# One padded column buffer, and the order of two transposes in front of the seventh pair, in a retention and mixture-of-experts kernel

## The chip, the cores and the metric

The kernel runs on one core of a Trainium2 chip. The metric is the device time of one launch in microseconds. Three runs of the kernel before took 415.46, 417.1 and 418.48 us; the median is 417.1 us.

## The reference

Two stages, all in float32. First a retention (linear attention) over 4 batches, 8 heads, 768 steps and head size 64:

```python
state = gamma * state + einsum('bhd,bhe->bhde', k[t], v[t])
y[t] = scale * einsum('bhd,bhde->bhe', q[t], state)
```

Its output is read as x, 3,072 tokens of 512 numbers. Then a mixture of 8 experts: each token goes to the expert with the largest logit x @ w_gate, and gets

```python
h = maximum(x[mask] @ w1[e], 0)            # 512 -> 1024
out[mask] = gate_w * sigmoid(x @ w_output_gate)[e] * (h @ w2[e])
```

## The kernel before, in words

**Attention, the first 125 us or so.** The 768 steps of a batch are cut into 6 chunks of 128. Two batches run beside each other, so the 24 chunks make 12 *pairs* (`for p in range(NCH // 2)`), the chunks of pair p being `n0 = 2p` and `n1 = 2p + 1`. Pairs 0 to 5 work on the first two batches, pairs 6 to 11 on the others. `nxt = p + 1`, and `NC` is 6, so `nxt == NC` holds once, at the end of the sixth pair (p = 5), in front of the seventh.

For each pair TensorE does, in this order: `inter` (queries by the state of the chunks before; left out where a batch starts, so in the seventh pair too), `scores` (L399, keys by queries), transposes of a part of the queries for a later pair, `tokens` (L529, outputs turned for the router), `values` (L417), `state` (L424, left out at a batch's last chunk), `counts` (L490 to L495), and then, for the next pair, `turn_keys` twice (L346) and `turn_queries` (L359), and at the end `logits` (L443). ScalarE copies most of the transposed tiles out of PSUM (`keep_keys`, `keep_queries`, both with L342, the line of the helper `copy`). With `nxt == NC` the second chunk's keys are copied by VectorE.

PSUM is handed out by hand: four banks `sp[0]` to `sp[3]`, named s0 to s3 below. Two habits matter here. `scores(n0)` of an even chunk writes banks s0 and s1, `scores(n1)` writes s2 and s3; the turned queries stand in s1 until ScalarE has copied them, the turned keys in s2 and s3; and the small sums of `gates` (VectorE, L516 to L520) stand in a corner of s0, since `gates(grp, bank[:, 6 * E:6 * E + 4])` is called with `bank = sp[0]`.

The order of each engine's instructions is the order of the program text (`tc.manual_schedule()`): no planner moves anything.

**Loads.** `load_k` (L273), `load_v` (L278), `load_q` (L283) and `first_queries` (L312) are issued by SyncE (queue 1), two by ScalarE at the start. A chunk of k or v is 256 KB: to each of 128 partitions, 8 heads of 64 floats, so 8 pieces of 256 bytes. `load_q` takes two chunks, in pieces of 512 bytes. Each waits for a free buffer (6 for k, 4 for v, 2 for q).

**Experts, from there to the end.** Tokens are sorted by expert through DRAM (`scatter`, L556), each expert's tokens are read back, split into a high and a low part (`xh`, `xw`) and multiplied with w1 (L1048), the result (`hh`, `hl`) with w2 (L1071, L1099). Weights come in slices of 512 KB into five buffers `raw`, each 1,056 floats = 4,224 bytes a partition, one behind the other: w1 as 4 pieces of 512 bytes per partition, w2 as one piece of 2,048. As 4,224 is 16 x 256 + 128, the five start by turns at a multiple of 256 bytes and 128 behind one.

**Where buffers lie.** The pools are stacked in the order in which they are opened: constants, weights, `hpool`, and behind it the attention's pools, and later, in the attention's place, the experts' pool. In `hpool` stand `col0` (7 numbers used, 32 taken), and behind it `idx0`, `tmp0` and `ot0`. Whatever lies behind `col0` moves if it grows; `raw`, `whi`, `wlo`, `xh0`, `xw0` and `h0` lie ahead of it.

Of the kernel before, what the change touches and what calls it, by code (L numbers as in the profile page):

```python
# [13 lines left out]
I32 = mybir.dt.int32  # L14
# [8 lines left out]
HEAD = 224  # L23
# [11 lines left out]
def retention_moe_kernel(  # L35
# [15 lines left out]
    P = 128  # L51
# [4 lines left out]
    NC = S // P  # L56
# [12 lines left out]
    hpool = ctx.enter_context(tc.tile_pool(name="hpool", bufs=1))  # L69
# [177 lines left out]
    with ExitStack() as actx:  # L247
# [6 lines left out]
        sp = [ps_s.tile([P, 512], F32, name=f"s{b}") for b in range(4)]  # L254
# [83 lines left out]
        def blocks(bank):  # L338
            return bank.rearrange("p (g t) -> p g t", g=NG)

        def copy(eng, dst, src):
            (eng.copy if eng is nc.scalar else eng.tensor_copy)(dst, src)  # L342

        def turn_keys(i, bank):
            for g in range(NG):
                nc.tensor.transpose(blocks(bank)[:, g], kn[i][:, 2 * g:2 * g + 2].rearrange("p h d -> p (h d)"), ident)  # L346

        def keep_keys(i, bank, eng=nc.scalar):
            kt[i] = ap.tile([P, NG, P], F32, name="kt", tag="kt", bufs=2)
            copy(eng, kt[i], blocks(bank))  # L350
# [5 lines left out]
        def turn_queries(ch, j, r, bank):  # L356
            src = qr.pop((ch, j, r))
            for g in range(NG):
                nc.tensor.transpose(blocks(bank)[:, g], src[:, 2 * g:2 * g + 2].rearrange("p h d -> p (h d)"), ident)  # L359
# [13 lines left out]
        def keep_queries(ch, j, r, bank, eng=nc.scalar):  # L373
            if r == 0:
                qt[ch, j] = ap.tile([P, NG, 2, P], F32, name="qt", tag=f"qt{ch}", bufs=2)
            copy(eng, qt[ch, j][:, :, r], blocks(bank))
# [108 lines left out]
        def counts(grp, bank):  # L485
            n = len(grp)
            oh = rt["oh"]
            cnt = bank[:, 0:n * E]
            rt["cnt"] = cnt
            nc.tensor.matmul(cnt, tri_b, oh.rearrange("p a e -> p (a e)"), start=True, stop=False, skip_group_check=True)  # L490
            for t in (cb, acc):
                nc.tensor.matmul(cnt.rearrange("p (a e) -> p a e", e=E), ones_b, t.unsqueeze(1).broadcast_to([P, n, E]),
                                 start=False, stop=True, skip_group_check=True)
            if n == 2:
                nc.tensor.matmul(cnt[:, E:2 * E], ones_b, oh[:, 0], start=False, stop=True, skip_group_check=True)  # L495

        def add_counts(grp, eng):
            for a in range(len(grp)):
                eng.tensor_tensor(out=acc, in0=acc, in1=rt["oh"][:, a], op=ALU.add)

        def route2(grp, bank):
            n = len(grp)
            oh = rt.pop("oh")
            rk = bank[:, 4 * E:6 * E].rearrange("p (a e) -> p a e", a=2)
            nc.vector.tensor_tensor(out=rk, in0=rt.pop("cnt").rearrange("p (a e) -> p a e", e=E), in1=oh, op=ALU.mult)
            pos = sm.tile([P, 2], I32, name="pos", tag="pos", bufs=4)[:, 0:n]
            with nc.allow_low_precision("row numbers are whole"):
                nc.vector.tensor_reduce(out=pos, in_=rk, axis=AX.X, op=ALU.add)  # L508
            for a, i in enumerate(grp):
                rt["pos", i] = pos[:, a:a + 1]  # L510

        def gates(grp, tmp):
            ex = rt.pop("ex")
            n = len(grp)
            se, den = tmp[:, 0:2], tmp[:, 2:4]
            nc.vector.tensor_reduce(out=se, in_=ex[:, :, 0:E], axis=AX.X, op=ALU.add)  # L516
            nc.vector.tensor_scalar(out=se, in0=se, scalar1=1e-9, scalar2=None, op0=ALU.add)
            nc.vector.scalar_tensor_tensor(out=den, in0=ex[:, :, E], scalar=1.0, in1=se, op0=ALU.add, op1=ALU.mult)
            gate = sm.tile([P, 2], F32, name="gate", tag="gate", bufs=3)[:, 0:n]
            nc.vector.reciprocal(gate, den)  # L520
            for a, i in enumerate(grp):
                rt["gate", i] = gate[:, a:a + 1]
# [31 lines left out]
        def scatter(i, last=False, mark=None):  # L554
            row = rt.pop(("row", i))
            s_ = nc.gpsimd.indirect_dma_start(  # L556
                out=srt, out_offset=bass.IndirectOffsetOnAxis(ap=rt.pop(("pos", i)), axis=0),
                in_=row.rearrange("p a x -> p (a x)"), in_offset=None, bounds_check=E * REG - 1, oob_is_err=False)
            wait_for(s_, mark)
            if not last:  # L560
                tc.declare_no_dep(s_.ins, group="srt", reason="rows are disjoint")
                tc.add_to_no_dep_group("srt", s_.ins)
            else:
                for o in sent:
                    tc.add_manual_dep(s_.ins, o.name, mybir.DependencyInfo(
                        mybir.DependencyClass.Sync, mybir.DependencyReason.DATA), reason="sorted rows complete")
            sent.append(s_.ins)
# [18 lines left out]
        hd = {}  # L586
# [18 lines left out]
            nc.gpsimd.tensor_sub(hd["xl"][:, 2 * g:2 * g + 2], tp, hd["xh"][:, 2 * g:2 * g + 2].bitcast(F32))  # L605

        def keep_ids():
            hd["c"] = hpool.tile([P, 32], I32, name="col0")[:, 0:HEAD // 32]
            nc.gpsimd.tensor_copy(hd["c"], hd["t"][:, :, P].bitcast(I32))

        def head_ids():
# [98 lines left out]
        for p in range(NCH // 2):  # L710
# [3 lines left out]
            nxt = p + 1  # L714
            ahead = (p % 2, p // 2 + 1) if 2 <= p < 2 * NQ - 2 else None
# [97 lines left out]
            if grp:  # L813
                bank = sp[3] if last else yp[0] if p == 1 else sp[0]
                counts(grp, bank)
                add_counts(grp, nc.gpsimd)
                if last:
                    for i in (n0 - 4, n0 - 3):
                        scatter(i)
                route2(grp, bank)  # L820
                gates(grp, bank[:, 6 * E:6 * E + 4])
            if n0 + 2 < NCH:
                turn_keys(n0 + 2, sp[2])
                keep_keys(n0 + 2, sp[2])
                turn_keys(n0 + 3, sp[3])
                keep_keys(n0 + 3, sp[3], nc.vector if nxt == NC else nc.scalar)
            if p == 1:
                for r in range(2):
                    turn_queries(1, 1, r, sp[r])
                    keep_queries(1, 1, r, sp[r])  # L830
            if ahead:
                turn_queries(*ahead, 1, sp[1])
                keep_queries(*ahead, 1, sp[1])
            if last:
# [29 lines left out]
            if p == 10:  # L864
                split_high(2)
                head_prep(0)
                head_prep(1)
                keep_ids()
# [448 lines left out]
```

## Time and profile before

| | |
|---|---|
| runs | 415.46, 417.1, 418.48 us |
| the profiled execution | 414.55 us, of which its span is 412.6 us |
| busy over the span | PE 97%, PEld 91%, DVE 54%, ACT 45%, POOL 63% |
| granted TensorE clock | full speed in nearly all slices of the span |
| moved by DMA | 75.75 MB, 184 GB/s over the span |

The span runs from the first to the last instruction of the profiled execution; 1.95 us lie around it. PE is TensorE's matmuls and PEld its weight loads, DVE is VectorE, ACT ScalarE, POOL GpSimd, SP SyncE. "L399" is line 399 of the kernel. `out<-in` names the tiles that an instruction writes and reads.

### The profile page before, as it was taken

To read this page: it belongs to the slowest core of one execution; us is meant where nothing else is said; L and a number is where in the kernel's file an instruction comes from. 1 tells how busy PE (TensorE), PEld (TensorE's weight loads), DVE (VectorE), ACT (ScalarE), POOL (GpSimd) and SP (SyncE) were. 2 spreads that over 40 slices of the span, in tenths; PEclk is the share of its full clock that TensorE was granted. 3 is DMA by queue.
4 is the path that set the end of the run, shared out by engine and by line. 5 is a ranking of instruction groups with operands and counts; after the bars stand their busy time and mean duration, and the time that the engine had idled before them with its cause. 6 is when DMAs were issued, how large, how long until landed. Compare 5 with 4: busy or idle time off the path is not lost.

```text
span 412.6 us, 10487 instructions
## 1 busy us (share of the span) xinstructions
PE 399.8 (97%) x3599; PEld 374.8 (91%) x3599; DVE 224.0 (54%) x558; ACT 184.7 (45%) x358; POOL 261.6 (63%) x323
## 2 busy tenths in 40 slices
PE   6799999999999999999999999999999999999994
PEld 3688888888889999999999999999999999999892
DVE  3466666676687866734553563554455465465120
ACT  2255555555576335633533543544444454353111
POOL 5354676554797227874357768786786887787532
PEclk9999999999999999999999999999999999999998
DMA  9999999879976489787596468459648756830102
GB/s 148 191 220 240 237 234 249 210 207 262 252 213 209 156 209 264 230 205 214 151 196 188 149 153 241 151 157 227 204 143 183 226 169 151 250 97 17 40 23 75
DMA packets 129277, 75.75 MB, mean 184 GB/s; under 512 B 60596, under 2 KB 117400, under 8 KB 129184
## 3 DMA queue, kind: packets, MB, share of 16 engines
q1 hardware_dynamic: 121136, 59.12, 60.3%
q0 software_dynamic: 5968, 14.84, 10.1%
q8 instruction: 61, 1.00, 1.0%
q10 hardware_dynamic: 2080, 0.52, 0.8%
q14 instruction: 32, 0.26, 0.2%
HBM read 59.71 MB, written 15.30 MB: 182 GB/s over the span
## 4 chain that ended last, share of the span: by engine, by line
PE 84%; DMA 5%; issue 3%; SPq 3%; POOL 2%; ACT 1%; POOLq 0%; ACTq 0%
PE h L1048 28%; PE a L1071 27%; PE s L399 5%; PE y L417 5%; PE s L529 3%; PE s L643 3%; PE y L623 2%; PE y L391 2%; PE s L346 2%; PE s L359 2%; DMA qn<-in_q_dram 2%; DMA out_dram<-ot,idi 2%; POOL out_dram L223 2%; PE st L424 2%; DMA kn<-in_k_dram 2%
## 5 line engine op out<-in xcount | busy, mean ns | idle before, releaser
L223 POOL DMA_INDIRECT out_dram<-ot,idi x86 | 86.7, 1008 | 28.7 <-issue 16.7
L202 POOL TENSOR_TENSOR wlo<-raw,whi 128x512 fp32r<-128x512 f32 x56 | 74.6, 1332 | 41.9 <-ACT whi L194 34.2
L1048 PE MATMUL h<-xh,whi 128*128 128x360 f32 (+5 forms) x256 | 84.3, 329 | 0.0
L1048 PE MATMUL h<-xh,wlo 128*128 128x360 f32 (+5 forms) x256 | 84.1, 328 | 0.0
L1048 PE MATMUL h<-xw,whi 128*128 128x360 f32 (+5 forms) x256 | 84.1, 328 | 0.0
L1058 DVE SCALAR_TENSOR_TENSOR hl<-h,hh 128x224 fp32r<-128x224 f32 (+7 forms) x64 | 35.8, 559 | 80.3 <-ACT hh L1057 77.1
L1071 PE MATMUL a<-hl,whi 128*128 128x392 f32 (+4 forms) x224 | 74.0, 330 | 0.0
L1071 PE MATMUL a<-hh,wlo 128*128 128x392 f32 (+4 forms) x224 | 73.9, 330 | 0.0
L1071 PE MATMUL a<-hh,whi 128*128 128x392 f32 (+4 forms) x224 | 73.8, 329 | 0.0
L1057 ACT ACTIVATE hh<-h 128x224 fp32r<-128x224 f32 (+7 forms) x64 | 31.4, 491 | 71.1 <-PE h L1048 71.1
L193 ACT CAST whi<-raw 128x512 fp32r<-128x512 f32 x64 | 39.6, 619 | 36.8 <-PE a L1071 26.8
L201 DVE TENSOR_TENSOR wlo<-raw,whi 128x512 fp32r<-128x512 f32 x56 | 38.9, 694 | 27.9 <-ACT whi L193 25.1
L1048 PEld LDWEIGHTS h<-xh,whi 128*128 128x128 f32 x256 | 48.2, 188 | 0.4
L1048 PEld LDWEIGHTS h<-xw,whi 128*128 128x128 f32 x256 | 48.2, 188 | 0.4
L1048 PEld LDWEIGHTS h<-xh,wlo 128*128 128x128 f32 x256 | 48.2, 188 | 0.2
L407 DVE TENSOR_TENSOR am<-s,mask 128x512 f32<-128x512 f32 x48 | 29.8, 684 | 31.1 <-PE s L399 31.1
L556 POOL DMA_INDIRECT srt<-row,pos x24 | 24.1, 1005 | 32.3 <-DVE pos L508 17.4
L1071 PEld LDWEIGHTS a<-hh,wlo 128*128 128x128 f32 x224 | 42.3, 189 | 0.2
L1071 PEld LDWEIGHTS a<-hh,whi 128*128 128x128 f32 x224 | 42.3, 189 | 0.1
L1071 PEld LDWEIGHTS a<-hl,whi 128*128 128x128 f32 x224 | 42.2, 188 | 0.1
L194 ACT CAST whi<-raw 128x512 fp32r<-128x512 f32 x64 | 39.5, 617 | 0.0
L981 ACT CAST xh<-xt 128x416 fp32r<-128x416 f32 (+2 forms) x28 | 15.1, 540 | 37.8 <-DVE xt L980 37.8
(215 smaller groups left out, 643.0 us busy)
## 6 DMA issues: line engine op xcount, KB each, us to landing
raw<-in_moe_w_dram SPq DMA_DIRECT2D x128, 128.0 KB
raw<-in_moe_w_dram SPq DMA_DIRECT2D x64, 256.0 KB
vn<-in_v_dram SPq DMA_DIRECT2D x24, 256.0 KB
kn<-in_k_dram SPq DMA_DIRECT2D x23, 256.0 KB
qn<-in_q_dram SPq DMA_DIRECT2D x10, 512.0 KB
xl<-srt SPq DMA_DIRECT2D x12, 209.6 KB
xl<-srt SPq DMA_DIRECT2D x8, 225.8 KB
xl<-srt SPq DMA_DIRECT2D x8, 193.5 KB
```

The source lines that it names most:

```text
L193: nc.scalar.copy(hi[:, 0], raw[:, 0])
L194: nc.scalar.copy(perm(hi), r2)
L201: (first or nc.vector).tensor_sub(lo[:, 0], raw[:, 0], hi[:, 0].bitcast(F32))
L202: (second or nc.gpsimd).tensor_sub(perm(lo), r2, perm(hi).bitcast(F32))
L223: st = nc.gpsimd.indirect_dma_start(out=dst, out_offset=bass.IndirectOffsetOnAxis(ap=idx, axis=0), in_=src, in_offset=None, bounds_check=n ...
L399: marks["scores"] = nc.tensor.matmul(sp[2 * (n % 2) + b][:, (2 * S_ + o) * P:(2 * S_ + o) * P + P], kt[n][rows(b), g], queries(n, g, b), s ...
L407: nc.vector.tensor_tensor(out=a.rearrange("p s o t -> p (s o) t"), in0=sp[2 * (n % 2) + b].rearrange("p (x t) -> p x t", t=P), in1=mask.un ...
L556: s_ = nc.gpsimd.indirect_dma_start(out=srt, out_offset=bass.IndirectOffsetOnAxis(ap=rt.pop(("pos", i)), axis=0), in_=row.rearrange("p a x ...
L1048: nc.tensor.matmul(ps[:, 0:C], l[:, 0, w], r[:, dc, 0:C], start=(n == 0), stop=(n == 3 * NDC - 1))
L1057: nc.scalar.activation(hh, ps[:, 0:C], AF.Relu)
L1058: marks["relu"] = nc.vector.scalar_tensor_tensor(out=hl, in0=ps[:, 0:C], scalar=0.0, in1=hh.bitcast(F32), op0=ALU.max, op1=ALU.subtract)
L1071: nc.tensor.matmul(accs[d][:, 0:C], l[:, 1, w], r[:, 0:C], start=(f == 0 and n == 0), stop=(f == NF - 1 and n == 2))
```

## The change

`col0` grows from 32 to 64 numbers per partition, from 128 to 256 bytes; still 7 of them are used. All that lies behind it moves up by 128 bytes. In the built program this puts the start of these tiles, as the rest by 256:

| tiles | before | after |
|---|---|---|
| kn, vn, qn, qr, qt, kt, vs, am, gn, gq, sd (attention) | 128 | 0 |
| hh, hl, ot (experts) | 128 | 0 |
| xh, xw, xt (experts), lt | 0 | 128 |
| the two buffers xl | 128, 192 | 0, 64 |
| the four buffers row | 128, 160, 192, 224 | 0, 32, 64, 96 |
| ot0 | 64 | 192 |

Second, with `nxt == NC`, the queries' transposes and their copy stand ahead of the keys'. In the other pairs nothing moves.

```diff
         def keep_ids():
-            hd["c"] = hpool.tile([P, 32], I32, name="col0")[:, 0:HEAD // 32]
+            hd["c"] = hpool.tile([P, 64], I32, name="col0")[:, 0:HEAD // 32]
...
                 gates(grp, bank[:, 6 * E:6 * E + 4])
+            if ahead and nxt == NC:
+                turn_queries(*ahead, 1, sp[1])
+                keep_queries(*ahead, 1, sp[1])
             if n0 + 2 < NCH:
                 turn_keys(n0 + 2, sp[2])
                 keep_keys(n0 + 2, sp[2])
...
-            if ahead:
+            if ahead and nxt != NC:
                 turn_queries(*ahead, 1, sp[1])
                 keep_queries(*ahead, 1, sp[1])
```

On TensorE, between the counts of the sixth pair and the scores of the seventh, there stood (s0 to s3 are the PSUM banks, kn a chunk's keys as loaded, qr a part of the queries, qt and kt their turned copies, yt outputs; in brackets the engine or the DMA queue that is waited for):

```order
L346 MATMUL s2_127<-ident_71,kn_890 128x128 [waits DMAHW3_49]
L346 MATMUL s2_127<-ident_71,kn_890 128x128 x3
L346 MATMUL s3_128<-ident_71,kn_896 128x128 [waits DMAHW6_49]
L346 MATMUL s3_128<-ident_71,kn_896 128x128 x3
L359 MATMUL s1_126<-ident_71,qr_1060 128x128 x4
L443 MATMUL misc_129<-yt_1165,wg_137 32x256 [waits DVE_49,Activation_49]
L443 MATMUL misc_129<-yt_1165,wg_137 32x256 [waits DVE_49]
L443 MATMUL misc_129<-yt_1165,wg_137 32x256 x2
L399 MATMUL s0_125<-qt_947,kt_1189 128x128 [waits DVE_49,Activation_49]
L399 MATMUL s1_126<-qt_947,kt_1189 128x128 [waits Activation_49]
```

and now stands:

```order
L359 MATMUL s1_126<-ident_71,qr_1060 128x128 x4
L346 MATMUL s2_127<-ident_71,kn_890 128x128 [waits DMAHW3_49]
L346 MATMUL s2_127<-ident_71,kn_890 128x128 x3
L346 MATMUL s3_128<-ident_71,kn_896 128x128 [waits DMAHW6_49]
L346 MATMUL s3_128<-ident_71,kn_896 128x128 x3
L443 MATMUL misc_129<-yt_1165,wg_137 32x256 [waits DVE_49,Activation_49]
L443 MATMUL misc_129<-yt_1165,wg_137 32x256 [waits DVE_49]
L443 MATMUL misc_129<-yt_1165,wg_137 32x256 x2
L399 MATMUL s0_125<-qt_947,kt_1194 128x128 [waits DVE_49,Activation_49]
L399 MATMUL s1_126<-qt_947,kt_1194 128x128
```

The four transposes of queries went ahead of the eight of keys; the first score still waits for VectorE and ScalarE, the second, which writes s1, for nothing more of its own.

On ScalarE, at the same place, there stood:

```order
L482 ACTIVATE ex_1147<-misc_129 128x18 [waits DVE_49]
L342 COPY kt_1189<-s2_127 128x512 [waits PE_49,Activation_49]
L342 COPY qt_1119<-s1_126 128x4x128 [waits PE_49]
L448 COPY lt_1206<-misc_129 128x256 [waits PE_49]
L342 COPY qr_1212<-qn_1066 128x512 [waits DMAHW2_49,Activation_49]
```

and now stands:

```order
L482 ACTIVATE ex_1147<-misc_129 128x18 [waits DVE_49]
L342 COPY qt_1119<-s1_126 128x4x128 [waits PE_49]
L342 COPY kt_1194<-s2_127 128x512 [waits PE_49,Activation_49]
L448 COPY lt_1206<-misc_129 128x256 [waits PE_49]
L342 COPY qr_1212<-qn_1066 128x512 [waits DMAHW2_49,Activation_49]
```

The copy of the queries went ahead of that of the first chunk's keys. VectorE, GpSimd and SyncE have their instructions in the order of before.

## Rows read from the trace of the kernel before

**Rows 1.** The page's parts 1 and 4: busy time by engine; the chain's shares.

```profile
PE 399.8 (97%) x3599; PEld 374.8 (91%) x3599; DVE 224.0 (54%) x558; ACT 184.7 (45%) x358; POOL 261.6 (63%) x323
...
PE 84%; DMA 5%; issue 3%; SPq 3%; POOL 2%; ACT 1%; POOLq 0%; ACTq 0%
```

**Rows 2.** Stretches: busy us per engine, then granted clock, DMA share, GB/s.

```profile
0.00:10.00 10.00, 6.72 (x36) 3.39 (x36) 3.75 (x9) 2.07 (x3) 5.12 (x16) 1.00 0.98 147
10.00:20.00 10.00, 7.30 (x118) 6.20 (x117) 4.47 (x7) 2.34 (x4) 3.32 (x4) 1.00 1.25 187
...
30.00:40.00 10.00, 9.79 (x165) 8.13 (x164) 5.74 (x17) 5.89 (x13) 4.79 (x14) 1.00 1.02 231
40.00:50.00 10.00, 10.00 (x169) 8.60 (x168) 6.33 (x21) 5.78 (x12) 5.92 (x9) 1.00 0.99 235
```

**Rows 3.** The chain of waits, first 45 us: start, length, what.

```profile
13.16 6.74 DMA kn<-in_k_dram
...
20.70 7.77 DMA qn<-in_q_dram
```

**Rows 4.** Waits of PE, 0 to 40 us: total, times, longest.

```profile
PE s L346 <- DMA kn<-in_k_dram: 2.4, 3, 1.4
...
PE y L346 <- DMA kn<-in_k_dram: 0.6, 1, 0.6
PE st L364 <- DMA qn<-in_q_dram: 0.6, 1, 0.6
PE s L364 <- DMA qn<-in_q_dram: 0.5, 1, 0.5
...
PE s L359 <- ACT qr L342: 0.4, 1, 0.4
```

**Rows 5.** Waits of PE, 40 to 125 us (the answer's only row).

```profile
PE s L399 <- ACT qt L342: 0.2, 1, 0.2
```

**Rows 6.** Timeline in front of the seventh pair: start, length, what, idle before.

```profile
68.80 1.07 PE L346 MATMUL s<-ident,kn 128*128 128x128 f32 x8
69.53 0.58 ACT L342 COPY kt<-s 128x512 f32<-128x512 f32 x1 [1.06 <-PE s L346]
69.71 0.60 PE L359 MATMUL s<-ident,qr 128*128 128x128 f32 x4
70.24 0.64 PE L443 MATMUL misc<-yt,wg 128*32 128x256 f32 x8
70.34 0.58 ACT L342 COPY qt<-s 128x512 f32<-128x512 f32 x1 [0.23 <-PE s L359]
70.74 0.17 DVE L520 RECIPROCAL gate<-s 128x2 f32<-128x2 f32 x1
70.83 0.67 DVE L342 COPY kt<-s 128x512 f32<-128x512 f32 x1
71.06 2.06 PE L399 MATMUL s<-qt,kt 64*128 64x128 f32 x32 [0.18 <-ACT qt L342]
```

**Rows 7.** DMA queue 1, at 10:20, then 30:40: packets, MB, share of 16 engines.

```profile
q1 hardware_dynamic: 6606, 1.86, 124.6%
...
q1 hardware_dynamic: 7793, 2.29, 101.2%
```

**Rows 8.** The same, one weight slice each: 227.4:232.5, 328.9:333.6, 296.0:301.2.

```profile
q1 hardware_dynamic: 684, 0.52, 34.5%
...
q1 hardware_dynamic: 686, 0.52, 37.4%
...
q1 hardware_dynamic: 681, 0.52, 34.0%
```

**Rows 9.** Groups of matmuls by shape: busy us, mean ns of one.

```profile
L1071 PE MATMUL a<-hl,whi 128*128 128x392 f32 x64 | 21.7, 340 | 0.0
...
L1048 PE MATMUL h<-xh,whi 128*128 128x392 f32 x64 | 21.7, 340 | 0.0
```

## The prediction

> **What bounds the kernel now.** I read the page first for the engine that fills the span, then the chain of waits for where that engine is held up, then PE's own waits stretch by stretch, since an edit that speeds something else is worth only what PE waits for it. PE is busy for 97% of the span and makes 84% of the chain; DMA makes 5% of it [rows 1]. So the kernel is TensorE's, apart from the start. The stretches show it: in the first two 10 us PE has work for 6.72 and 7.30 us, from 30 us on for 9.79 and then all of it [rows 2]. The chain's two long DMA pieces, a load of keys of 6.74 us and one of queries of 7.77 us, also lie there [rows 3]. What PE loses to loads in the first 40 us is 2.4 + 0.6 + 0.6 + 0.5 = 4.1 us, and 0.4 us more through the copy qr, which waits for a load of queries [rows 4]. From 40 to 125 us, the rest of the attention, PE has a single wait, 0.2 us at L399 [rows 5]; it is the one in front of the seventh pair. The two edits aim at just these: the addresses at the loads, the swap at that 0.2 us. At most 4.5 + 0.2 us, 1.1% of the time, could come back.
>
> **The swap.** It adds no instruction; four transposes and one copy change places. Before, the eight transposes of keys start at 68.80 us and the four of queries at 69.71 us; the queries' copy runs from 70.34 to 70.92 us, and the first score starts at 71.06 us, 0.18 us idle behind it, because it writes bank s1, in which the queries stood [rows 6]. Now the queries come first. Their transposes take 0.60 us from 68.80 us; the copy can start where the keys' copy started, at 69.53 us, ends 0.58 us later at 70.11 us, and the keys' copy behind it at 70.69 us. So ScalarE lets the first score go 0.23 us sooner.
>
> But that score also waits for VectorE, since `gates` keeps its sums in s0, which the score writes too. The reciprocal L520 is the last to touch s0; it runs from 70.74 to 70.91 us [rows 6], and nothing ahead of it on VectorE has moved. The old wait ended at 70.92 us, the new one ends at 70.91 us: 0.01 us is gained. This wait was hidden under the other; that is what is late next. The bounds are 0 and the whole idle of 0.2 us [rows 5]; I take 0, because the two ends are read from the same rows. A loss would need the keys' copy to end after 70.92 us, and it has 0.23 us to spare. The second chunk's keys are copied by VectorE behind L520, at 70.83 us as before, and their transposes end at about 68.80 + 0.60 + 1.07 = 70.47 us, in time; that copy ends at 71.50 us, before the second half of the scores (71.06 + 2.06 / 2 = 72.09 us) wants it. No DMA is issued or passed in the swap, and GpSimd's and SyncE's queues stay as they are.
>
> **The addresses, for the engines.** The padding itself costs nothing: the copy into `col0` still has 7 columns, and no instruction is added. What moves is the start of operands. TensorE shows both cases side by side: L1048 reads `xh` and `xw`, which start at a multiple of 256 bytes, L1071 reads `hh` and `hl`, which start 128 behind one. At equal width, 392 columns, both take 340 ns [rows 9]. The change swaps them. Were the difference a whole nanosecond, the last place of the rows, 768 matmuls of L1048 against 672 of L1071 would leave 96 ns. I take 0.
>
> **The addresses, for the loads.** This is the term that decides. No row shows a piece of 256 bytes that lands at a multiple of 256, since kn, vn and qn all start 128 behind one. The nearest rows are the weight slices, for their buffers alternate. Mean time per packet is share x 16 engines x stretch / packets: slice 31, at a multiple, 0.345 x 16 x 5.1 us / 684 = 41.2 ns; slice 55, at a multiple too, 0.374 x 16 x 4.7 / 686 = 41.0 ns; slice 47, 128 behind, 0.340 x 16 x 5.2 / 681 = 41.5 ns [rows 8]. That is 0.4 ns or 1% for the better place, hardly more than two equal places differ by. On the 20 us at the start in which PE waits for loads, 1% is 0.2 us, and I take that.
>
> The outer bound for a gain comes from the start itself. At 10 to 20 us a packet of queue 1 takes 1.246 x 16 x 10 / 6606 = 30.2 ns, at 30 to 40 us 1.012 x 16 x 10 / 7793 = 20.8 ns [rows 7], and the rates are 187 and 231 GB/s [rows 2]. If it were the place that slows the start, both halves of it would come up to 231 GB/s: 19% of 20 us, 3.8 us, less than the 4.5 us that PE has to give. Against that speaks that kn and vn lie at the same places at 30 to 40 us, and go fast. For a loss, the same 1% the other way is 0.2 us; nothing in the rows sets an end farther out but that of the slower rival below.
>
> The Trainium skill has a rule for this: "DMA: Bandwidth & Descriptors", section "How a descriptor splits into AXI transactions", says that a transaction has to start at a multiple of 256 bytes, so that a descriptor which starts elsewhere moves bytes it does not use. By its beats of 32 bytes a piece of 512 bytes that starts 128 behind costs 20 beats against 16, and one of 256 bytes 12 against 8; taken so for the place where a load lands, it would be the first rival's time. The slices of rows 8 do not show that step, though their pieces of 512 bytes would have it.
>
> The scatter's tiles `row` and the results `ot` are read by DMAs from new places too; PE waits for neither in the stretches read, so I set 0, with the loads' 1% of a transfer as the bound on both sides.
>
> **The sum**, on the profiled execution's own 414.55 us: 0 for the swap, 0 for the engines, 0.2 us for the loads: 414.35 us. That execution is 2.55 us below the median of the runs shown, 417.1 us, and below all three. On the median the sum is 417.1 - 0.2 = **416.9 us**. The three runs spread over 3 us, so about 1.5 us either way is what runs of one kernel do, and a change of 1%, 4.2 us, is about what can be told from none.
>
> **The rivals.**
>
> *The place does slow the start.* Then queue 1 at 10 to 20 us goes at the rate of 30 to 40 us, and PE's waits of rows 4 shrink by 3.8 us: 417.1 - 3.8 = 413.3 us. For it: the chain lies on just these loads [rows 3], and pieces of 256 bytes, nowhere seen at a multiple, may feel it where 512 do not. Against it: rows 8, and the fast packets at the old places in rows 7. Chance 0.12.
>
> *The even place is worse for loads, and the time gets longer.* All of kn, vn and qn now start at the same place within 256 bytes as aligned writes, on all partitions. If each packet of queue 1 took longer by some share, the start would be late by that share of 20 us, and the stretch from 20 to 75 us, where the queue has no room (its share is 101.2% at 30 to 40 us [rows 7], and the DMA share is still 0.99 at 40 to 50 us [rows 2]), by that share of some 40 us once the six buffers of keys are used up. It decides from 4.2 / 60 = 7% on; at 10% it is 6 us, 423 us. Against it: the slices at even places take no more than the others [rows 8]. Chance 0.04.
>
> *The swap does nothing at all* is part of my forecast, not a rival; that it does all it could, 0.2 us, would not be seen in the time.
>
> **How the numbers follow.** The forecast, that PE-bound work stays as it is and the loads as good as keep their pace, gets 0.80 and 415.2 to 418.5 us. The first rival gets 0.12, with 413.3 us, just inside the 1% (412.9 us); its spread puts about a third of it, 0.04, below. The slower one gets 0.04, and 0.04 is left for a wandering of the measurement, half of it each way, of which half is beyond 1%. Faster by over 1%: 0.04 + 0.01 = 0.05. Slower: 0.04 + 0.01 = 0.05. Within 1%: 0.90. The range for 8 in 10 reaches from the forecast's own to the first rival's time, and a little above the slowest run: 413.3 to 418.8 us.
>
> **What would show it.** In the profile of the changed kernel the first score of the seventh pair should start within 0.05 us of where it did, counted from the first of the transposes (2.26 us after it), and its wait be put down to VectorE's L520 or to ScalarE's kt. If it starts 0.2 us sooner, the hidden wait was misread. PE's waits for loads in the first 40 us should again sum to 4 us or so, and queue 1 at 10 to 20 us to about 30 ns a packet; if the sum falls to 1 us and the packet to 21 ns, the first rival holds. If PE gets waits for kn, qr or vs after 40 us, the slower one does. L1048 and L1071 should keep 340 ns at 392 columns. The prediction is wrong if the median leaves 413.3 to 418.8 us, or if a wait that no row here has comes up in the experts' stage.

## The result, and the profile after

The changed kernel takes 411.97 us (median of 6 runs, 409.99 to 412.76) against 417.32 us beside it: a ratio of 0.9867, 95% interval 0.9836 to 0.9898. That is 5.4 us or 1.3% faster, 1.3 us below the range of the prediction, and even below the price of its first rival, though that rival named the mechanism.

In the two profiles all of it is at the start. The page's parts 1 and 4 of the changed kernel: the chain no longer goes through a load at the start; 2% of DMA are left, from the last sends. No engine's own work got shorter: each one's busy time is within 0.2 us of [rows 1].

```profile
PE 400.0 (98%) x3599; PEld 374.8 (92%) x3599; DVE 223.8 (55%) x558; ACT 184.8 (45%) x358; POOL 261.8 (64%) x323
...
PE 90%; issue 3%; POOL 2%; DMA 2%; DVE 1%; POOLq 0%; ACT 0%; DVEq 0%; ACTq 0%
```

The same stretches as [rows 2] (us busy per engine, clock, DMA share, GB/s): PE now has work for 8.51 and 9.93 us of the first two 10 us, where it had 6.72 and 7.30, and loads move 188 and 248 GB/s in place of 147 and 187.

```profile
0.00:10.00 10.00, 8.51 (x48) 4.61 (x50) 3.65 (x9) 2.56 (x4) 6.45 (x18) 1.00 0.82 188
10.00:20.00 10.00, 9.93 (x182) 8.49 (x180) 4.89 (x8) 3.10 (x6) 4.91 (x5) 1.00 1.09 248
...
30.00:40.00 10.00, 9.96 (x169) 8.50 (x166) 6.37 (x22) 5.69 (x11) 4.41 (x9) 1.00 0.95 235
```

PE's waits in the first 40 us, the whole answer. The five rows of [rows 4], 4.5 us together, are gone; the 1.3 us of L168 is the start-up, which was there before as well. Not every profile with the new places has lost all of them: one wait for keys (L346) is left in the profiles of e2, e4 and e10 below, of 0.9, 0.5 and 1.2 us.

```profile
PE misc L168 <- DVE warm L90: 1.3, 1, 1.3
PE s L399 <- ACT kt L342: 0.2, 1, 0.2
```

Queue 1 at 10 to 20 us (packets, MB, share of 16 engines): 1.089 x 16 x 10 / 8483 = 20.5 ns a packet, where [rows 7] gave 30.2 ns. These are the two signs by which the prediction would know its first rival.

```profile
q1 hardware_dynamic: 8483, 2.46, 108.9%
```

By the scores of the third pair the gain is complete. The chain of waits (start, length, what), first of the changed kernel, then of the one before:

```profile
28.13 1.99 PE s L399 x32
```

```profile
32.91 1.99 PE s L399 x32
```

That is 4.78 us. Up to there PE does the same 364 matmuls in both; first the changed kernel, then the one before:

```profile
0.00:28.13 28.13, 26.55 (x364) 20.06 (x364) 14.19 (x36) 11.29 (x22) 15.88 (x35) 1.00 0.95 224
```

```profile
0.00:32.91 32.91, 26.41 (x364) 19.54 (x364) 14.42 (x36) 11.50 (x22) 16.00 (x35) 1.00 1.07 192
```

PE is idle for 28.13 - 26.55 = 1.58 us in place of 32.91 - 26.41 = 6.50 us: the gain is idle time of PE. The spans differ by 412.6 - 408.0 = 4.6 us, so what the start gives, PE keeps to the end. The medians differ by 0.7 us more than these two executions; the runs of one kernel spread over 3 us, and where the 0.7 us lie is open.

In front of the seventh pair (start, length, what, idle before) the first score comes 66.26 - 64.01 = 2.25 us after the first of the transposes, against 71.06 - 68.80 = 2.26 us in [rows 6], and the wait is now put down to VectorE's L520:

```profile
64.01 0.63 PE L359 MATMUL s<-ident,qr 128*128 128x128 f32 x4
64.48 1.04 PE L346 MATMUL s<-ident,kn 128*128 128x128 f32 x8
65.45 0.64 PE L443 MATMUL misc<-yt,wg 128*32 128x256 f32 x8
...
65.94 0.17 DVE L520 RECIPROCAL gate<-s 128x2 f32<-128x2 f32 x1
...
66.26 2.06 PE L399 MATMUL s<-qt,kt 64*128 64x128 f32 x32 [0.17 <-DVE gate L520]
```

The matmuls at 392 columns (busy us, mean ns of one) take 336 to 340 ns in all twelve groups, six before and six after, though xh has left its multiple of 256 and hl has reached one. Two of them answer to [rows 9]; L1051 and L1074 are what L1048 and L1071 were before:

```profile
L1051 PE MATMUL h<-xh,whi 128*128 128x392 f32 x64 | 21.7, 339 | 0.0
...
L1074 PE MATMUL a<-hl,whi 128*128 128x392 f32 x64 | 21.6, 337 | 0.0
```

### The profile page after: what moved, and what is told of

Same layout as the page of the kernel before. It is cut to its first block, busy times and chain, and to the rows that moved or that the text cites. A ratio compares the mean times of both kernels' runs of the same rounds, so it can differ in the third digit from the quotient of the medians.

```text
span 408.0 us, 10488 instructions
## 1 busy us (share of the span) xinstructions
PE 400.0 (98%) x3599; PEld 374.8 (92%) x3599; DVE 223.8 (55%) x558; ACT 184.8 (45%) x358; POOL 261.8 (64%) x323
## 4 chain that ended last, share of the span: by engine, by line
PE 90%; issue 3%; POOL 2%; DMA 2%; DVE 1%; POOLq 0%; ACT 0%; DVEq 0%; ACTq 0%
PE h L1051 28%; PE a L1074 28%; PE s L399 6%; PE y L417 6%; PE s L529 3%; PE s L643 3%; PE y L391 3%; PE y L623 2%; PE s L359 2%; PE s L346 2%; PE st L424 2%; DMA out_dram<-ot,idi 2%; POOL out_dram L223 2%; PE misc L443 2%; PE misc L168 1%
## 5 line engine op out<-in xcount | busy, mean ns | idle before, releaser
L223 POOL DMA_INDIRECT out_dram<-ot,idi x86 | 86.7, 1008 | 28.5 <-issue 18.5
L1051 PE MATMUL h<-xw,whi 128*128 128x360 f32 (+5 forms) x256 | 84.1, 328 | 0.0
L1051 PE MATMUL h<-xh,wlo 128*128 128x360 f32 (+5 forms) x256 | 84.0, 328 | 0.0
L1051 PE MATMUL h<-xh,whi 128*128 128x360 f32 (+5 forms) x256 | 84.0, 328 | 0.0
L1074 PE MATMUL a<-hl,whi 128*128 128x392 f32 (+4 forms) x224 | 73.9, 330 | 0.0
L1074 PE MATMUL a<-hh,whi 128*128 128x392 f32 (+4 forms) x224 | 73.9, 330 | 0.0
L1074 PE MATMUL a<-hh,wlo 128*128 128x392 f32 (+4 forms) x224 | 73.5, 328 | 0.0
L1051 PEld LDWEIGHTS h<-xh,whi 128*128 128x128 f32 x256 | 48.2, 188 | 0.4
L1051 PEld LDWEIGHTS h<-xw,whi 128*128 128x128 f32 x256 | 48.2, 188 | 0.4
L1051 PEld LDWEIGHTS h<-xh,wlo 128*128 128x128 f32 x256 | 48.2, 188 | 0.2
L407 DVE TENSOR_TENSOR am<-s,mask 128x512 f32<-128x512 f32 x48 | 29.8, 683 | 27.2 <-PE s L399 25.5
L1074 PEld LDWEIGHTS a<-hh,whi 128*128 128x128 f32 x224 | 42.2, 188 | 0.4 <-issue 0.2
L1074 PEld LDWEIGHTS a<-hl,whi 128*128 128x128 f32 x224 | 42.2, 188 | 0.3
L1074 PEld LDWEIGHTS a<-hh,wlo 128*128 128x128 f32 x224 | 42.2, 188 | 0.2
```

What stands on the lines that cost most here:

```text
L223: st = nc.gpsimd.indirect_dma_start(out=dst, out_offset=bass.IndirectOffsetOnAxis(ap=idx, axis=0), in_=src, in_offset=None, bounds_check=n ...
L407: nc.vector.tensor_tensor(out=a.rearrange("p s o t -> p (s o) t"), in0=sp[2 * (n % 2) + b].rearrange("p (x t) -> p x t", t=P), in1=mask.un ...
L1051: nc.tensor.matmul(ps[:, 0:C], l[:, 0, w], r[:, dc, 0:C], start=(n == 0), stop=(n == 3 * NDC - 1))
L1074: nc.tensor.matmul(accs[d][:, 0:C], l[:, 1, w], r[:, 0:C], start=(f == 0 and n == 0), stop=(f == NF - 1 and n == 2))
```

## The experiments

"Even" below is a start at a multiple of 256 bytes, "odd" any other. Each run's ratio is to the kernel before, run beside it.

**Which edit.** e1 is the changed kernel with `col0` at 32 numbers again, e2 the kernel before with it at 64 (the edit shown; e1's is its reverse).

```diff
-            hd["c"] = hpool.tile([P, 32], I32, name="col0")[:, 0:HEAD // 32]
+            hd["c"] = hpool.tile([P, 64], I32, name="col0")[:, 0:HEAD // 32]
```

> Swap alone, the column buffer at its old 128 bytes. Theory A (the whole gain comes from where the loads of k, v and q land): 417 us, as before (416 to 418.5), PE's waits for loads in the first 40 us again about 4 us, the first score of the seventh pair held by VectorE's L520 for 0.2 us. Theory B (the swap brings a part): 414 to 416 us.

> Padding alone, the old order in front of the seventh pair. Theory A: 412 us (410.5 to 413), no PE wait for a load in the first 40 us, and the 0.2 us at the seventh pair's first score put down to ScalarE's copy of the queries again. Theory B: 413.5 us or more.

e1: 416.42 us, ratio 0.9987 (0.9947 to 1.0026). e2: 412.17 us, ratio 0.9874 (0.9806 to 0.9942). The padding brings the gain, the swap nothing that can be measured. PE's waits from 40 to 125 us say why; of e1, then of e2, the whole answers:

```profile
PE s L529 <- DVE am L407: 0.4, 1, 0.4
PE s L399 <- DVE gate L520: 0.2, 1, 0.2
```

```profile
PE s L529 <- DVE am L407: 0.7, 1, 0.7
PE s L399 <- ACT qt L342: 0.2, 1, 0.2
```

With the swap the score's wait is put down to the reciprocal, without it to the copy, and it is as long. The wait at L529 comes with either place and is in neither of the two profiles compared above. Two expectations were missed in part: e1's waits for loads in the first 40 us sum to 3.1 us, not about 4, and e2 keeps one of 0.9 us where none was expected.

**Odd or moved.** e3 gives `col0` 48 numbers: everything behind it moves by 64 bytes, to another odd place.

```diff
-            hd["c"] = hpool.tile([P, 32], I32, name="col0")[:, 0:HEAD // 32]
+            hd["c"] = hpool.tile([P, 48], I32, name="col0")[:, 0:HEAD // 32]
```

> The column buffer of 192 bytes: all behind it moves by 64 bytes, so kn, vn and qn start 192 behind a multiple of 256; old order. Theory A, that a piece of 256 bytes is slow where it crosses a multiple of 256: as slow as before, 416 to 418.5 us, since every piece still crosses one. Theory C, that any other place than the old one would do (a matter of how buffers lie to each other, or of multiples of 128): 410.5 to 413 us.

418.02 us, ratio 1.0021 (0.9987 to 1.0056). Theory C falls: moving buffers is not enough, a piece at 192 is as slow as one at 128. Queue 1 at 10 to 20 us has 1.237 x 16 x 10 / 6617 = 29.9 ns a packet:

```profile
q1 hardware_dynamic: 6617, 1.86, 123.7%
```

**Which tiles.** e4 pads the attention's pool in place of `hpool`; e5 and e6 put a gap between the queries' load buffers and the rest (e6 with e4's padding too).

```diff
-        fill_up(ac, 8)
+        fill_up(ac, 40)          # e4, e6
...
         first_queries(1, 0)
+        ap.tile([P, 32], F32, name="gap", tag="gap", bufs=1)   # e5, e6
         load_k(0, nc.scalar)
```

> 128 bytes more behind the attention's small constants in place of the column buffer: kn, vn, qn, qt, kt, vs, am, qr, sd and row start at a multiple of 256, while gn, gq and all of the experts' tiles (hh, hl, ot, xh, xw, xl) stay where they were; old order. Theory A: 412 us (410.5 to 413). Theory D, that part of the gain is the experts' tiles or gn: 413.5 us or more.

> 128 bytes between the queries' load buffers and those of keys and values: kn, vn (and the attention tiles behind them) start at a multiple of 256, qn and the first queries' buffers 128 behind, gn and the experts' tiles as before; old order. If the keys' and values' loads (pieces of 256 bytes) carry the gain: 411 to 413.5 us. If the queries' loads do: 415.5 to 418 us.

> The counterpart: qn and the first queries' buffers start at a multiple of 256, kn, vn and all attention tiles behind them 128 behind; old order. If keys and values carry the gain: 414.5 to 417.5 us. If the queries do: 411 to 413.5 us.

e4: 410.52 us, ratio 0.9879 (0.9802 to 0.9956): the whole gain without the experts' tiles, which stay where they were; theory D falls. e5: 413.6 us, 0.9936 (0.9903 to 0.997), just above what was expected. e6: 415.17 us, 0.9981 (0.9954 to 1.0007), as expected, and not told from nothing. So keys and values carry about half of it, 0.64% of 1.21%; the time of the queries alone shows nothing certain. Whether the two add up to e4 cannot be told from these times, for e4's interval reaches from 0.44 to 1.98%. The profiles suggest that they do: the first copy qr, which waits for the first whole load of queries, starts at 21.29 us in e5 and 22.62 us in e6, against 23.9 us with all buffers odd and 19.9 us with all attention buffers even (the means worked out below). That is 2.6 and 1.3 us of 4.0, from one profile each.

**The disputed cost by itself.** e7, e8 and e9 compute nothing: SyncE issues loads of 256 KB (of 512 KB where the pieces are 512 bytes), phase behind phase, each into fresh buffers at a given place. Up to eight may be in flight; SyncE has four or five of 256 KB under way at a time, but in phase 4 of e7 two. Each of e7, e8 and e9, and of e11 and e12 below, was run once. The line that picks the source is shortened:

```python
for i, (b, c) in enumerate(loads):
    t = pool.tile([P, H, one * D], F32, name=f"t{n}", tag=f"t{n}", bufs=bufs)   # bufs = 2: two in flight
    ...
    nc.sync.dma_start(t, t_src[b, :, c * P:(c + 1) * P, :].rearrange("h p d -> p h d"))
```

> Loads alone, no computing, the output is zeros: four phases one behind the other, each 24 loads of 256 KB in pieces of 256 bytes, issued by SyncE. Phase 1: places 128 behind a multiple of 256, up to eight loads in flight; phase 2: at a multiple, eight in flight; phase 3: 64 behind, eight in flight; phase 4: 128 behind, two buffers only, so two in flight. Theory A with crowding (a piece that crosses a multiple of 256 is slow only with many loads in flight): phases 1 and 3 about 30 ns a packet and 40 us long, phase 2 18 to 20 ns and 28 us, phase 4 18 to 20 ns a packet. Theory A without crowding: phase 4 as slow a packet as phase 1. Theory E (it is the first 20 us of a launch that are slow, at odd places): phase 1 30 ns, phases 2, 3 and 4 all 18 to 20 ns.

> Loads alone, no computing, the output is zeros. Phase 1: 24 loads of 256 KB, pieces of 256 bytes at a multiple of 256; phase 2: the same, 128 behind; phase 3: 12 loads of 512 KB, pieces of 512 bytes, 128 behind; phase 4: the same at a multiple; up to eight loads in flight throughout. Theory A: phase 1 18 to 20 ns a packet, phase 2 about 30 ns though it is not at the start; phase 3 above phase 4 by a smaller share. Theory E: phases 1 and 2 alike, 3 and 4 alike.

Queue 1 in the middle of each phase of e7, at 6:30, 36:57, 66:87 and 96:126 us:

```profile
q1 hardware_dynamic: 20731, 5.23, 134.9%
...
q1 hardware_dynamic: 20633, 5.20, 109.4%
...
q1 hardware_dynamic: 18141, 4.58, 137.5%
...
q1 hardware_dynamic: 21353, 5.38, 78.8%
```

Share x 16 x stretch / packets gives 25.0 ns at 128, 17.8 ns at 0, 25.5 ns at 64, and 17.7 ns at 128 with two in flight. And e8, at 6:26, 33:57, 63:81 and 87:102 us:

```profile
q1 hardware_dynamic: 19908, 5.02, 110.9%
...
q1 hardware_dynamic: 20717, 5.22, 134.9%
...
q1 hardware_dynamic: 10365, 5.23, 119.8%
...
q1 hardware_dynamic: 10315, 5.20, 114.9%
```

That is 17.8 ns at 0, 25.0 ns at 128; with pieces of 512 bytes 33.3 ns at 128 and 26.7 ns at 0. Theory E falls, since the odd phase is slow in either order. With four or five loads in flight an odd place makes a packet about 7 ns longer, of 256 as of 512 bytes, and at 64 as much as at 128. The expected size, 30 ns, was too high.

A packet's time is not the rate: a share above 100% says that an engine has more than one packet in hand on average, so packets overlap. The rate falls from 248 to 251 to 218 GB/s for pieces of 256 bytes and from 347 to 291 GB/s for 512. Per engine (16 x stretch / packets) that is one packet every 18.5 ns in place of 16.1 to 16.3 ns, and every 27.8 ns in place of 23.3 ns: a loss of 2.2 to 2.5 and of 4.5 ns.

With two loads in flight (79%) an odd packet takes no longer than an even one with four or five. No even phase with two in flight was run, so that the price is then nothing is not shown. The kernels themselves bear out that it is small. At 60 to 70 us queue 1 has, in the kernel before and in the changed one:

```profile
q1 hardware_dynamic: 5065, 1.54, 64.2%
...
q1 hardware_dynamic: 5949, 1.77, 74.7%
```

That is 20.3 and 20.1 ns. In the same way e1 and e3, odd, have 21.3 and 20.9 ns, and e2 and e4, even, 19.6 and 20.0 ns: about 0.9 ns between the means, where the start has 30.2 against 20.5 ns. What in the fuller queue makes an odd place dearer is not shown.

**What else makes the start slow.** 25 ns is less than the 30.2 ns of [rows 7]. e9 tries loads into half of the partitions (the first queries' kind) and keys and values by turns:

```python
nc.sync.dma_start(half[o * 64:o * 64 + 64] ..., q[b, :, c * P:c * P + P, :].rearrange("h (p r) d -> p r h d", r=2))  # 1, 2
nc.sync.dma_start(t, (k if i % 4 < 2 else v)[..., :, (i // 4) * P:(i // 4 + 1) * P, :].rearrange("h p d -> p h d"))     # 3, 4
```

> Loads alone, no computing, the output is zeros; up to eight loads in flight. Phases 1 and 2: 24 loads of the first queries' kind (256 KB into 64 partitions, the lower and the upper half by turns), first 128 behind a multiple of 256, then at one. Phases 3 and 4: 24 loads of keys and values by turns (two of keys, two of values, as at the kernel's start), 128 behind, then at a multiple. If loads into half of the partitions are what makes the odd place dearer at the kernel's start than the 25 ns of loads alone: phase 1 32 ns a packet or more, phase 2 18 to 22 ns. If the mixture of keys and values is: phase 3 32 ns or more, phase 4 18 to 20 ns. If neither: 25 ns in phases 1 and 3, and what makes the start dearer is something else that runs there.

At 6:32, 36:62, 69:92 and 96:119 us:

```profile
q1 hardware_dynamic: 21045, 5.31, 132.3%
...
q1 hardware_dynamic: 24473, 6.17, 117.4%
...
q1 hardware_dynamic: 19854, 5.01, 134.7%
...
q1 hardware_dynamic: 22333, 5.63, 108.1%
```

26.2 ns odd and 20.0 ns even for half of the partitions, 25.0 and 17.8 ns for the mixture: neither reaches the 32 ns that would have named it. e11 then issues the kernel's first fifteen loads in their order, odd, even, odd, even, and e12 adds GpSimd's six.

```python
fq(0, 0, nc.scalar); fq(1, 0); one(kn, k, 0, nc.scalar); one(kn, k, 1); one(vn, v, 0); one(vn, v, 1)
# then gn twice, fq(0, 1), fq(1, 1), kn 2, kn 3, vn 2, vn 3, and the first whole load of queries
nc.gpsimd.dma_start(gv, ...); nc.gpsimd.dma_start(ga, ...)     # e12; and four of wg
```

> Loads alone, no computing, the output is zeros: the kernel's first fifteen loads in their order (first queries, keys, values, the decays gn to half of the partitions from one source row, the next keys and values, the first whole load of queries), two of them issued by ScalarE as there; phase 1 places 128 behind a multiple of 256, phase 2 at one, phase 3 as 1, phase 4 as 2, each behind the one before. If the loads themselves make the kernel's start as slow as it was (30 ns a packet at 10 to 20 us): phases 1 and 3 take about 18 to 20 us each from first to last landing, with stretches of 30 ns and more, phases 2 and 4 14 to 16 us. If what computes beside them adds to it: phases 1 and 3 stay at 25 to 27 ns, 16 to 17 us.

> As e11, with the kernel's six loads by GpSimd (gv, ga and four of wg, in pieces of 192 and 32 bytes) beside the fifteen; odd place, even place, odd, even. Loads alone lost about 2.5 us at the odd place in e11, the whole kernel lost 4.5 us. If GpSimd's small loads make the rest: phases 1 and 3 take 22 us or more, phases 2 and 4 18 us. If not: 21 and 18 us as in e11, and the rest is something that computes or fetches beside them.

Stretches from the first issue to the landing of the last load, phase by phase (length first, DMA share and GB/s last); e11, then e12:

```profile
0.72:21.35 20.63, 0.00 (x0) 0.00 (x0) 1.00 1.10 191
21.73:40.09 18.36, 0.09 (x2) 0.00 (x0) 1.00 0.94 214
40.47:61.45 20.98, 0.09 (x3) 0.00 (x0) 1.00 1.13 187
61.82:79.79 17.97, 0.57 (x3) 0.00 (x0) 1.00 0.96 219
```

```profile
0.74:22.78 22.04, 0.00 (x1) 3.74 (x6) 1.00 1.15 182
23.21:42.29 19.08, 0.09 (x2) 3.57 (x6) 1.00 0.94 210
42.72:64.22 21.50, 0.10 (x3) 3.56 (x6) 1.00 1.13 187
64.65:83.75 19.10, 0.58 (x3) 3.56 (x6) 1.00 0.94 210
```

The odd place costs these loads 2.3 and 3.0 us in e11, 3.0 and 2.4 us in e12; GpSimd's loads lengthen odd and even phases alike (by 0.5 to 1.4 us), so they are not the rest; but e12's first odd phase, 22.0 us, reached the bound that was set for the opposite. The even phases, 18.0 and 18.4 us in e11 and 19.1 us in e12, took longer than the 14 to 16 and the 18 us expected. At 10 to 20 us queue 1 has, in e11, then in e12:

```profile
q1 hardware_dynamic: 7300, 2.18, 126.9%
...
q1 hardware_dynamic: 7191, 2.02, 133.6%
```

That is 27.8 and 29.7 ns a packet, where the kernels with all buffers odd have 30.2, 27.4 and 29.9 ns (before, e1, e3). So its own loads, in their order and kinds, reach nearly the packet time of the start with nothing computing beside them. In the whole kernel the first copy qr, which waits for the last of these loads, starts at 24.24, 23.32 and 24.19 us in the profiles with all buffers odd (before, e1, e3) and at 19.49, 20.07, 19.32 and 20.79 us with all attention buffers even (after, e2, e4, e10): means of 23.9 and 19.9 us, 4.0 us apart. So about 2.7 us of 4.0, the mean of the four differences, are the loads by themselves. Some 1.3 us come only with the computing kernel around them; the size is rough, as the profiles of either group lie up to 1.5 us apart, and what makes them stays open.

**The hidden wait.** e10 is the changed kernel with the sixth pair's counts and gates in the state's bank, so that the score needs nothing from VectorE.

```diff
-                bank = sp[3] if last else yp[0] if p == 1 else sp[0]
+                bank = sp[3] if last else yp[0] if p == 1 else st[:, 0] if nxt == NC else sp[0]
```

> The changed kernel, with the sixth pair's counts and gates in the state's bank instead of s0, so that the seventh pair's first score waits for VectorE no longer. If L520 was the hidden wait behind the copy of the queries: no PE wait put down to L520 between 40 and 125 us, and the first score starts 0.1 to 0.25 us sooner after the first of the transposes than the changed kernel's; the time stays at 411 to 413 us. If something else holds the score: the 0.2 us stay under another name.

PE has no wait at all from 40 to 125 us, and the score comes 66.95 - 64.94 = 2.01 us after the first transposes, 0.24 us sooner than in the changed kernel:

```profile
64.94 0.64 PE L359 MATMUL s<-ident,qr 128*128 128x128 f32 x4
...
66.95 2.06 PE L399 MATMUL s<-qt,kt 64*128 64x128 f32 x32
```

One run took 411.18 us; 0.24 us cannot be seen in a time. So L520 was the wait behind the wait.

## Why the prediction was wrong

**Right: what bounds the kernel, the swap, the engines.** The time lay where PE waited for loads in the first 40 us; after that nothing gave way. The swap is worth 0.01 us in the profile, as forecast, and without the wait for L520 the score comes 0.24 us sooner (e10). The places of matmul operands cost nothing that shows. One reading was off on the way. The prediction has the first score wait for the queries' copy because it writes s1; in the order shown ahead of it the first score writes s0, and only the second writes s1. The first score starts 71.06 - 70.91 = 0.15 us after L520's end in [rows 6] and 66.26 - 66.11 = 0.15 us after it in the changed kernel. So L520 held it already, the copy ended within 0.01 us of it, and the profile named the later one.

**Wrong: "The addresses, for the loads. ... That is 0.4 ns or 1% for the better place."** The step took the price of an odd place from the weight slices [rows 8], whose shares are 34 to 37%, and carried it to the start, where the share is 125% [rows 7]. There the better place is worth 30.2 - 20.5 = 9.7 ns a packet or 32%, and the term of 0.2 us came out at 4.6 us in the profiles' spans. The price depends on how full the queue is: e7 shows 17.7 ns with two loads in flight (a share of 79%) and 25.0 ns with four or five (135%), at one and the same odd place. The weights' rows were measured with a queue that was mostly empty, and could hardly have shown it. The share stood beside each of those rows and was used in the division only.

**Wrong: the bound.** 3.8 us came from the rate at 30 to 40 us, 231 GB/s, taken as what an undisturbed queue does. Those loads were odd too. In e7 and e8 an odd place keeps pieces of 256 bytes at 218 GB/s, an even one at 248 to 251, and the changed kernel moves 248 GB/s at 10 to 20 us. The evidence against the rival, "fast packets at the old places", was read from a stretch with less in flight, at a share of 101%.

**The first rival's chance.** I gave it 0.12 because rows 8 seemed to contradict it; with a share of a third they said little about it. The prediction set beside it the rule of the Trainium skill, "DMA: Bandwidth & Descriptors", section "How a descriptor splits into AXI transactions", which is told there for the bytes that a descriptor fetches. By that rule, as an estimate, a piece of 256 or 512 bytes that does not start at a multiple of 256 makes one transaction more, and one of 256 bytes makes 10 beats when it starts at 64 and 12 at 128, against 8. For the place where a load lands the runs agree that such a start costs. They do not follow the beats, for 64 costs as much as 128 (25.5 and 25.0 ns). One price for one more transaction fits the packet times (about 7 ns for either size) and not the rates (2.2 to 2.5 and 4.5 ns). So the runs show the cost, and not what in the engine makes it.

**The size.** The rival's 413.3 us was 1.3 us too high. Its bound of 3.8 us was too low, as said. Of PE's idle time 4.92 us went: the five waits of rows 4, 4.5 us, and most of the rest is another 0.5 us in which L417 waited for `am` in the kernel before. The prediction's 4.5 us of what PE has to give left that wait out. PE's own work ahead of the third pair's scores took 0.14 us longer, which leaves the 4.78 us. That GpSimd's small loads were part of it was looked for and not found (e12).

## What to carry to other kernels

Give every buffer that a crowded queue fills in pieces of 256 or 512 bytes a start at a multiple of 256 bytes: one odd-sized small tile ahead of them moves them all off. And take the price of a transfer from a row whose queue is as full as the one it is meant for; a row with a share of a third says little about a start at 125%. Packets in a crowded queue overlap, so compare rates too before giving one a price. Where two waits end within 0.01 us of each other, removing one is worth nothing until the other goes.

## What the runs showed of the hardware

Late loads can come with a lower granted clock as well. In e1 the stretches (busy us per engine, granted clock, DMA share, GB/s) at 10 to 20 and 20 to 30 us are these:

```profile
10.00:20.00 10.00, 7.44 (x112) 6.16 (x110) 4.47 (x7) 1.76 (x3) 3.14 (x3) 0.93 1.22 202
20.00:30.00 10.00, 10.00 (x145) 8.51 (x146) 4.51 (x14) 4.39 (x9) 4.40 (x11) 0.73 1.06 236
```

In the first of them PE had work for 7.44 us, and the clock began to fall; in part of the next it ran at the lower of its two levels, 1.2 GHz, and the scores at 22.99 us took 3.19 us, where they take 2.06 us at the higher level:

```profile
22.99 3.19 PE L399 MATMUL s<-qt,kt 64*128 64x128 f32 x32
```

e6 shows the same, 0.89 and 0.77, and e3 0.93 at 0 to 10 and 0.90 at 10 to 20 us. In e1 PE is busy for 402.7 us, 2.9 us longer than before. The profiles of after, e2, e4 and e10 have 1.00 in all these stretches, and so has the one of before, where PE waited no less: the fall comes in some executions.

The runs say the same over the whole span. The mean granted clock is 0.995 to 0.999 in all 14 runs of after, e2 and e4, and 0.987 to 0.998 in the 19 runs of the kernel before beside e1 to e4. That this fall makes part of the gain is not shown: of these 19, the 8 with 0.996 or more took 414.5 to 418.4 us, the others 414.6 to 419.3 us.
